# A cross-covariance attention and gated FFN kernel: the second chunk of v transposed by DMA, with four smaller moves

## The chip, the core and the metric

The kernel runs on one core of one Trainium2 chip. The metric is device time in microseconds of one execution. The core has a matrix engine (TensorE, PE in the profile, its weight loads shown as PEld), VectorE (DVE), ScalarE (ACT), GpSimd (POOL) and SyncE (SP), each with its own instruction queue that runs in order. Transfers are issued from a queue (here POOL's, SP's, at the start and the end also ACT's) and carried out by 16 DMA engines. Matmuls write to PSUM, which holds eight banks of 128 x 512 float32 values; the kernel's pools hand these banks out.

## What is computed

```python
B, N, C = 4, 6016, 256          # DFF = 1536
def _attn_ref(q, k, v, tau):
    qn = q / (np.linalg.norm(q, axis=1, keepdims=True) + 1e-06)
    kn = k / (np.linalg.norm(k, axis=1, keepdims=True) + 1e-06)
    s = kn.transpose(0, 2, 1) @ qn / tau
    s = s - s.max(-1, keepdims=True)
    a = np.exp(s)
    a /= a.sum(-1, keepdims=True) + 1e-09
    return v @ a

def _moe_ref(x, w_gate, w_val, w_out):
    gate = 1.0 / (1.0 + np.exp(-(x @ w_gate)))
    return gate * (x @ w_val) @ w_out
```

The second function is applied to the rows of the first one's result. Attention is over channels: for each of four batches one 256 x 256 matrix `a` comes from the whole of q and k, and then every row of v goes through `a` and through the gated FFN. Inputs and output are float32.

## The kernel before

**Stages.** For a batch, scores (`score`, tile ps_s) add up over 47 row tiles of 128 rows; the squares of q and k add up beside them for the norms. Then come the norms, their inverses, the exponentials (`e_sb`) and the row sums. `a` is never applied to v: `gh` multiplies the exponentials with the two weight matrices, giving G and H (12 pieces of 128 x 512, six tiles gh_G0..2 and gh_H0..2), and scales them by the row sums. After that each chunk of four row tiles (512 rows; 12 chunks a batch, the last with three tiles) runs 12 slots. One slot (`glu`) is two matmuls for the gate (ps_gate), two for the value (ps_val), a tanh on ScalarE (g_sb, L501) and one VectorE instruction that makes a slice of hT (L502). The output product of a chunk runs in the slots of the next chunk (`run_work`); all but the first chunk use a scheme of seven products of sums, whose sums VectorE makes (L524, in slots 1, 3, 4, 5, 6 and 7 to 11 of a chunk) and whose results ScalarE copies and GpSimd adds up (L578 to L580, L585, L595, L596). Most matmuls go through one helper, so their line is L127.

**Order.** The order is written out by hand (`manual_schedule`). In the main loop, a slot first issues `glu`, then the sums and a share of the output product, and then the side work that `side_work` has put down for this slot number. Slot numbers count from the start of a batch, 12 a chunk. The side work of a batch holds the loads and transposes of the coming chunks of v, and the whole preparation of the next batch: its loads, scores and squares up to slot 96, then, from `s0` = 98, its norms (`norms_mm`, `root_seed`, `root_steps`), inversion (`norms_inv`, L352 and L353 on VectorE), the spread of the inverse along columns (`spread_both`, four float32 matmuls into ps_rk), a copy of that on ScalarE (`copy_rk`, L315), the scaling of the scores (`scale_x`, L291, two halves), the exponentials (`exps`), the row sums and `gh`.

**The opening.** Batch 0 has nothing to overlap with. POOL's queue issues the loads of q and k (`load_qk`), then the first chunk of v (`load_v(0, 0)`, L178), six pieces of w_gate and w_val (L184), the second chunk of v (L188) and w_out (L195). After the last scores and the norms, TensorE's queue holds: two spreads into ps_rk, eight transposes of the first chunk of v against an identity (L468, tile ps_tp in a bank of the pool psv), the row sum of the first half of the exponentials, the first `gh`, the other row sum, three more `gh` (the second two in psv), and the first `glu`. VectorE copies one half of ps_tp to SBUF (L475), ScalarE the other (L723); the inversion of the first row sum stands ahead of VectorE's half, by way of the `then` argument of `transpose_v`.

**Transposes of v.** Each chunk of v is needed transposed (vT). Chunks from the third on are transposed by a DMA that SP issues (L465, DMA_TRANSPOSE), put down in slot 2 of the chunk before. The second chunk is transposed on TensorE in slot 8 of the first chunk, into a bank of the pool psm, and copied by one VectorE instruction.

**Banks.** Pools psg (ps_gate), psv (ps_val) and pso (ps_o) have two banks each, pss (the scores ps_s) and psm (small things) one.

Of the kernel before, what the change touches and what calls it, by code (L numbers as in the profile page):

```python
# [10 lines left out]
BF16 = mybir.dt.bfloat16  # L11
# [42 lines left out]
def kernel(  # L54
# [21 lines left out]
    P = nc.NUM_PARTITIONS  # L76
# [4 lines left out]
    B, N, C = q.shape  # L81
# [3 lines left out]
    CB = C // P  # L85
# [3 lines left out]
    TPC = 4  # L89
# [7 lines left out]
    def rows(x, b):  # L97
        return x[b].rearrange("(p t) c -> p t c", p=P)
# [3 lines left out]
    def pool(name, bufs, **kw):  # L102
        return ctx.enter_context(tc.tile_pool(name=name, bufs=bufs, **kw))
# [15 lines left out]
    psv = pool("psv", 2, space=PSUM)  # L119
    pso = pool("pso", 2, space=PSUM)  # L120
    pss = pool("pss", 1, space=PSUM)
    psm = pool("psm", 1, space=PSUM)
# [3 lines left out]
    def mm(out, lhsT, rhs, start, stop, **kw):  # L126
        nc.tensor.matmul(out, lhsT=lhsT, rhs=rhs, start=start, stop=stop, **kw)  # L127
# [4 lines left out]
    def load_qk(b, t0, nt):  # L132

        tiles = []
        for name, src in (("q", q), ("k", k)):
            tl = qkpool.tile([P, 2 * TPC, C], BF16, tag=name, name=name + "_sb")
            nc.gpsimd.dma_start(out=tl[:, :nt, :], in_=rows(src, b)[:, t0 : t0 + nt, :])
            tiles.append(tl)
        for u in range(0, nt, TPC):
            qk[b, t0 + u] = [tl[:, u : u + TPC, :] for tl in tiles]  # L140
# [3 lines left out]
    def load_v(b, ci):  # L144
        t0, nt = groups[ci]
        v_sb = vpool.tile([P, TPC, C], BF16, tag="v", name="v_sb")
        nc.gpsimd.dma_start(out=v_sb[:, :nt, :], in_=rows(v, b)[:, t0 : t0 + nt, :])
        vs[b, ci] = v_sb
# [26 lines left out]
    nc.scalar.copy(qk[0, 0][1], first_f32[1])  # L175
    for t0, nt in loads0[1:]:
        load_qk(0, t0, nt)
    load_v(0, 0)  # L178

    w_sb = [[consts.tile([P, CB, FG], BF16, name=f"w_{n}{fg}") for fg in range(NFG)] for n in ("gate", "val")]  # L180
    w_out_sb = consts.tile([P, FC, C], BF16)
    for fg in range(NFG):
        for w, src in enumerate((moe_w_gate, moe_w_val)):
            nc.gpsimd.dma_start(  # L184
                out=w_sb[w][fg],
                in_=src.rearrange("(t p) f -> p t f", p=P)[:, :, ds(fg * FG, FG)],
            )
    load_v(0, 1)  # L188

    w_sums = consts.tile([P, len(B_SUMS), FC // 2, P], BF16)  # L190
# [24 lines left out]
    def invert(out, x, eps, num):  # L215
        nc.vector.tensor_scalar(out=out, in0=x, scalar1=eps, scalar2=None, op0=ALU.add)
        nc.vector.reciprocal(out, out)
# [179 lines left out]
    def row_sums(b, i0, ni, pl, tag):  # L397
        s = st[b]
        ps_r = pl.tile([P, ni], FP32, tag=tag, name="ps_r")
        for i in range(ni):  # L400
            for j in range(CB):
                mm(
                    ps_r[:, i : i + 1],
                    s["e"][i0 + i][:, j, :],
                    ones_bf[:, 0:1],
                    start=(i == 0 and j == 0),
                    stop=(j == CB - 1),
                    skip_group_check=True,
                )
        r = attp.tile([P, ni], FP32, tag=f"rrow{i0}", name="rrow", bufs=2)  # L410
        invert(r, ps_r, 1e-9, 1.0)
        s.setdefault("rrow", []).extend(r[:, i : i + 1] for i in range(ni))
# [6 lines left out]
    def gh_tiles(b):  # L419
        st[b]["gh"] = [  # L420
            [ghpool.tile([P, CB, FG], BF16, tag=f"{n}{fg}", name=f"gh_{n}{fg}") for fg in range(NFG)]
            for n in ("G", "H")
        ]
# [28 lines left out]
    def gh(b, n, pl, tag, act=None):  # L452
        gh_store(b, n, gh_mms(b, n, pl, tag), n % 2 == 0 if act is None else act)
# [1 line left out]

    vts = {}

    def transpose_v(b, ci, ps=None, late=None, then=None):

        t0, nt = groups[ci]  # L460
        v_sb = vs.pop((b, ci))
        vT = vtpool.tile([P, TPC * CB, P], BF16, tag="vT", name="vT")
        flat = v_sb[:, :nt, :].rearrange("p t c -> p (t c)")
        if ps is None:
            nc.sync.dma_start_transpose(out=vT[:, : nt * CB, :], in_=flat)  # L465
        else:
            for n in range(nt * CB):
                nc.tensor.transpose(  # L468
                    out=ps[:, n, :], in_=flat[:, ds(n * P, P)], identity=ident_bf
                )  # L470
            half = nt * CB // 2 if late else nt * CB
            if late:
                late(vT[:, half : nt * CB, :], ps[:, half : nt * CB, :])
                then()
            nc.vector.tensor_copy(out=vT[:, :half, :], in_=ps[:, :half, :])  # L475
        vts[b, ci] = vT.rearrange("p (u cb) n -> p cb u n", cb=CB)

# [203 lines left out]
    for g, (t0, nt) in enumerate(groups0):  # L681
# [6 lines left out]
        while adds:  # L688
            w, last_sq = adds.pop()
# [26 lines left out]
    weights(0, 0)  # L716
    weights(0, 1)
    late = []
    ps_tp = psv.tile([P, TPC * CB, P], BF16, tag="v", name="ps_tp")
    gh_tiles(0)  # L720
    transpose_v(0, 0, ps_tp, lambda *a: late.append(a), lambda: row_sums(0, 0, 1, psm, "m"))
    gh(0, 0, psg, "g", act=True)
    nc.scalar.copy(*late.pop())  # L723
    half_row(0)
# [6 lines left out]
    def side_work(b):  # L731


        side = {}

        def at(slot, fn, *a):
            side.setdefault(divmod(slot, FC), []).append((fn, a))

        for ci in range(NCH):
            nb, nci = (b, ci + 1) if ci + 1 < NCH else (b + 1, 0)  # L740
            lb, lci = (b, ci + 2) if ci + 2 < NCH else (b + 1, ci + 2 - NCH)
            if (nb, nci) == (0, 1):
                at(8, lambda: transpose_v(0, 1, psm.tile([P, TPC * CB, P], BF16, tag="m", name="ps_tp")))
            elif nb < B:
                at(ci * FC + 2, transpose_v, nb, nci)
            if lb < B:
                at(ci * FC + 0, load_v, lb, lci)
            if (b, ci) == (0, 0):
                for i in range(FC // TPC):
                    at(8, copy_w_out, i)  # L750
                for n, m in enumerate((1, 0, 3, 2, 4)):
                    for i in range(FC // TPC):
                        at(10 + 2 * n, sum_w_out, m, i)
        n = b + 1
        if n == B:
            return side
        first, last = (14 if b == 0 else 0), 8 * FC
        for g, (t0, nt) in enumerate(groups):
            s0 = first + g * (last - first) // NCH
            if b == 0:  # L760
                at(max(0, s0 - 12), load_qk, n, t0, nt)
            elif s0 >= 24:
                at(s0 - 24, load_qk, n, t0, nt)
            for u in range(nt):
                at(first + (t0 + u) * (last - first) // NT, score, n, t0, u)
            if g == 0:
                at(s0, acc_start, n)
            for i, (fn, w) in enumerate(((acc_square, 0), (acc_add, 0), (acc_square, 1), (acc_add, 1))):
                at(s0 + 1 + 2 * i, fn, n, g, w)
        if n + 1 < B:  # L770
            for g, (t0, nt) in enumerate(groups[:3]):
                at(NCH * FC - 24 + 8 * g, load_qk, n + 1, t0, nt)
        s0 = 8 * FC + 2
        at(s0, norms_mm, n)
        at(s0 + 1, root_seed, n)
        at(s0 + 1, root_steps, n)
        at(s0 + 9, norms_inv, n)
        at(s0 + 10, spread_both, n)
        at(s0 + 11, copy_rk, n)
        at(s0 + 12, scale_x, n, 0)  # L780
        at(s0 + 13, scale_x, n, 1)
        at(s0 + 14, exps, n, 0)
        at(s0 + 15, exps, n, 1)
        at(s0 + 17, row_sums, n, 0, CB, psm, "m")
        at(s0 + 19, half_row, n)
        at(s0 + 17, gh_tiles, n)
        for i in range(len(gh_order)):
            at(s0 + 18 + 5 * i // 2, gh, n, i, *((pss, "s"), (psm, "m"))[i % 2])
        return side
# [68 lines left out]
```

## Time and profile before

| | |
|---|---|
| median of 4 runs | 809.05 us (808.88 to 809.21) |
| the profiled execution | 808.88 us |
| its span, first to last instruction | 807.1 us |
| mean granted TensorE clock | 0.998 |
| busy: PE, DVE, ACT, POOL | 786.7, 708.9, 525.7, 355.6 us |
| stretch 39 to 47 us: PE, DVE busy | 7.94, 6.57 of 8 us |
| stretch 47 to 56 us: PE, DVE busy | 9.00, 7.09 of 9 us |

The span runs from the first to the last instruction; the time of the execution also has what lies around it, 1.8 us here. A line of the timeline gives the start in us from the beginning of the span, the duration in us, the engine, the source line, the operation, out<-in, the shapes and the number of merged instructions, and in brackets how long the engine was idle before and what ended that. The end of a matmul is modelled and overlaps the next one's start; what TensorE loses is therefore read from the starts of matmuls, gate to gate. In a list of waits a line gives who waited for whom, us in total, times, and the longest. In the DMA view the number at the end of a line is the time from issue to landing.

### The profile page before, as it was taken

How to read it: one execution, taken by the hardware profiler on the slowest of the kernel's cores; microseconds unless marked ns; L12 is line 12 of the kernel's file. 1: busy time of each engine (PE TensorE's matmuls, PEld its weight loads, DVE VectorE, ACT ScalarE, POOL GpSimd, SP SyncE). 2: the span in 40 equal slices, each digit the busy share in tenths (PEclk: the TensorE clock that was granted, in tenths of full speed). 3: DMA queues.
4: the chain of work that ended last, by engine and by line, in shares of the span. 5: the costliest groups of instructions: out<-in, count | busy, mean ns of one | idle time of the engine just before them, and what ended most of it. 6: DMA issues, size and time to landing. Idle time of an engine off the chain costs nothing.

```text
span 807.1 us, 17902 instructions
## 1 busy us (share of the span) xinstructions
PE 786.7 (97%) x6776; PEld 501.0 (62%) x6776; DVE 708.9 (88%) x1202; ACT 525.7 (65%) x891; POOL 355.6 (44%) x566
## 2 busy tenths in 40 slices
PE   4899999999999999999999999999999999999998
PEld 2556666666666666666666666666666566666666
DVE  5777999999879999998987999999988898898896
ACT  3667777766667776775666767776666665665664
POOL 4473545444552454335343544443534244444433
PEclk9999999999999999999999999999999999999999
DMA  9997759432567557422367486524222332432312
GB/s 214 206 207 98 129 93 139 94 67 47 104 128 125 86 108 139 86 53 67 72 119 131 75 142 112 105 54 91 62 53 54 86 66 61 86 65 66 79 34 74
DMA packets 77319, 78.24 MB, mean 97 GB/s; under 512 B 50736, under 2 KB 55088, under 8 KB 77232
## 3 DMA queue, kind: packets, MB, share of 16 engines
q0 software_dynamic: 21648, 39.59, 30.0%
q1 hardware_dynamic: 55008, 36.64, 20.3%
q8 instruction: 53, 0.87, 0.4%
q10 hardware_dynamic: 576, 0.85, 0.3%
q14 instruction: 34, 0.28, 0.1%
HBM read 78.64 MB, written 24.64 MB: 128 GB/s over the span
## 4 chain that ended last, share of the span: by engine, by line
PE 92%; DMA 4%; DVE 2%; ACT 1%; issue 1%; POOL 0%; POOLq 0%
PE ps_gate L127 29%; PE ps_val L127 29%; PE ps_o L127 27%; PE ps_s L127 4%; DMA k_sb<-in_k_dram 3%; PE ps_gh L127 2%; DMA w_gate<-in_moe_w_gate_dram 1%; DVE hT L502 1%; DVE sums L524 0%; ACT g_sb L501 0%; PE ps_rk L127 0%; DVE r L352 0%; DVE acc L278 0%; PE ps_end L127 0%; PE ps_n L127 0%
## 5 line engine op out<-in xcount | busy, mean ns | idle before, releaser
L501 ACT ACTIVATE g_sb<-ps_gate 128x512 f32<-128x512 f32 (+1 forms) x576 | 338.3, 588 | 228.5 <-PE ps_gate L127 220.6
L502 DVE SCALAR_TENSOR_TENSOR hT<-g_sb,ps_val 128x512 bf16<-128x512 f32 (+1 forms) x576 | 384.8, 671 | 79.2 <-ACT g_sb L501 69.6
L127 PE MATMUL ps_val<-vT,gh_H 128*128 128x512 bf16 (+1 forms) x1152 | 337.5, 375 | 0.3 <-DVE hT L502 0.3
L127 PE MATMUL ps_gate<-vT,gh_G 128*128 128x512 bf16 (+1 forms) x1152 | 337.5, 375 | 0.0
L524 DVE TENSOR_TENSOR sums<-hT 128x768 bf16<-128x768 bf16 (+1 forms) x460 | 278.0, 604 | 0.0
L127 PEld LDWEIGHTS <-sums 128*128 128x128 bf16 x2670 | 183.0, 98 | 82.1
L127 PEld LDWEIGHTS <-gh_H 128*128 128x128 bf16 x1152 | 112.7, 98 | 131.6 <-issue 0.8
L595 POOL TENSOR_TENSOR out_sb<-out_sb,m_sb 128x256 f32<-128x256 f32 x89 | 78.6, 884 | 234.1 <-ACT out_sb L585 205.5
L127 PE MATMUL ps_o<-w_sums,sums 128*128 128x128 bf16 x1602 | 154.4, 219 | 0.0
L127 PEld LDWEIGHTS <-hT 128*128 128x128 bf16 x1200 | 88.3, 98 | 46.8
L579 POOL TENSOR_TENSOR m_sb<-m_sb 128x128 f32<-128x128 f32 x89 | 42.2, 474 | 166.0 <-ACT m_sb L578 166.0
L127 PEld LDWEIGHTS <-gh_G 128*128 128x128 bf16 x1152 | 97.0, 98 | 14.9
L127 PE MATMUL ps_o<-w_out_sb,sums 128*128 128x128 bf16 x1068 | 96.2, 219 | 0.0
L127 PE MATMUL ps_o<-w_sums,hT 128*128 128x128 bf16 x1068 | 95.5, 219 | 0.0
L127 PE MATMUL ps_s<-k_sb,q_sb 128*128 128x256 bf16 x376 | 70.7, 292 | 13.7 <-DMA k_sb<-in_k_dram 6.9
L596 POOL TENSOR_TENSOR out_sb<-out_sb 128x256 f32<-128x256 f32 x89 | 76.5, 859 | 7.0
L585 ACT COPY out_sb<-ps_o 128x512 f32<-128x512 f32 x89 | 52.2, 586 | 12.7 <-PE ps_o L127 10.1
L278 DVE TENSOR_TENSOR acc<-acc,sq 128x1024 bf16<-128x1024 bf16 (+1 forms) x66 | 59.8, 906 | 0.0
L580 POOL TENSOR_TENSOR m_sb<-m_sb 128x128 f32<-128x128 f32 x89 | 54.4, 612 | 7.0
L240 ACT ACTIVATE sq<-k_sb 128x1024 bf16<-128x1024 bf16 (+2 forms) x44 | 44.8, 1027 | 12.0 <-DMA k_sb<-in_k_dram 12.0
L127 PEld LDWEIGHTS <-q_sb 128*128 128x128 bf16 x376 | 33.7, 104 | 19.8 <-issue 9.5
L578 ACT COPY m_sb<-ps_o 128x384 f32<-128x384 f32 x89 | 42.6, 479 | 3.4 <-PE ps_o L127 1.0
(78 smaller groups left out, 306.5 us busy)
## 6 DMA issues: line engine op xcount, KB each, us to landing
out_dram<-out_sb SPq DMA_DIRECT2D x43, 512.0 KB, 3.4
v_sb<-in_v_dram POOLq DMA_DIRECT2D x44, 256.0 KB, 5.3
q_sb<-in_q_dram POOLq DMA_DIRECT2D x35, 256.0 KB, 4.9
k_sb<-in_k_dram POOLq DMA_DIRECT2D x35, 256.0 KB, 7.0
q_sb<-in_q_dram POOLq DMA_DIRECT2D x4, 512.0 KB, 11.4
k_sb<-in_k_dram POOLq DMA_DIRECT2D x4, 512.0 KB, 13.3
w_f<-in_moe_w_out_dram POOLq DMA_DIRECT2D x3, 512.0 KB, 10.6
out_dram<-out_sb SPq DMA_DIRECT2D x3, 384.0 KB, 2.8
```

Of the source, the lines that this page charges most:

```text
L127: nc.tensor.matmul(out, lhsT=lhsT, rhs=rhs, start=start, stop=stop, **kw)
L240: nc.scalar.activation(out=sq[:, :nt, :], in_=src[:, :nt, :], func=ACT.Square)
L278: nc.vector.tensor_tensor(out=acc[:, :nt, :], in0=acc[:, :nt, :], in1=st[b]["sq", w][:, :nt, :], op=ALU.add)
L501: nc.scalar.activation(out=g_sb[:, :n], in_=ps_gate[:, :n], func=ACT.Tanh, scale=0.5)
L502: nc.vector.scalar_tensor_tensor(out=hts[b, ci][:, f, :n], in0=g_sb[:, :n], scalar=1.0, in1=ps_val[:, :n], op0=ALU.add, op1=ALU.mult,)
L524: nc.vector.tensor_tensor(out=sums[b, ci, g][:, m, :, : half * P], in0=hT[:, f0 + k0 : f1 : 2, ds(r0 * half * P, half * P)], in1=hT[:, f0 ...
L578: nc.scalar.copy(m, states[p]["ps"][:, : 3 * P].rearrange("p (n c) -> p n c", c=P))
L579: nc.gpsimd.tensor_tensor(out=m[:, 1, :], in0=m[:, 1, :], in1=m[:, 2, :], op=ALU.add)
L580: nc.gpsimd.tensor_tensor(out=m[:, 2, :], in0=m[:, 1, :], in1=m[:, 0, :], op=ALU.add)
L585: nc.scalar.copy(o[:, p : p + half + 1 : half, :], states[p]["ps"].rearrange("p (t c) -> p t c", c=C),)
L595: add(out=ends, in0=ends, in1=states[p]["m"][:, 1:3, :], op=ALU.add)
L596: add(out=ends, in0=ends, in1=mids, op=ALU.subtract)
```

## The change

It has five parts.

- The second chunk of v is transposed by DMA like the later ones, from slot 2 of the first chunk, and not by TensorE in slot 8.
- In the opening, POOL issues the first piece of w_gate ahead of the first chunk of v.
- The first chunk's transposes write to the bank of the pool pss (which ps_s held) and not to one of psv.
- The row sum of the first half, and so its inversion on VectorE, is issued after the first half of the copy of ps_tp, and not before it.
- For batches 1 to 3, inversion, spread and the copy of the spread come one slot later; the first half of the scaling moves from s0 + 12 to s0 + 13, where the second half is.

```diff
@@ opening, loads @@
-    load_v(0, 0)
...
             nc.gpsimd.dma_start(
                 out=w_sb[w][fg],
                 in_=src.rearrange("(t p) f -> p t f", p=P)[:, :, ds(fg * FG, FG)],
             )
+            if fg == 0 and w == 0:
+                load_v(0, 0)
     load_v(0, 1)
@@ transpose_v @@
-    def transpose_v(b, ci, ps=None, late=None, then=None):
+    def transpose_v(b, ci, ps=None, late=None):
...
             if late:
                 late(vT[:, half : nt * CB, :], ps[:, half : nt * CB, :])
-                then()
             nc.vector.tensor_copy(out=vT[:, :half, :], in_=ps[:, :half, :])
@@ opening, transposes @@
-    ps_tp = psv.tile([P, TPC * CB, P], BF16, tag="v", name="ps_tp")
+    ps_tp = pss.tile([P, TPC * CB, P], BF16, tag="s", name="ps_tp")
     gh_tiles(0)
-    transpose_v(0, 0, ps_tp, lambda *a: late.append(a), lambda: row_sums(0, 0, 1, psm, "m"))
+    transpose_v(0, 0, ps_tp, lambda *a: late.append(a))
+    row_sums(0, 0, 1, psm, "m")
     gh(0, 0, psg, "g", act=True)
@@ side_work @@
-            if (nb, nci) == (0, 1):
-                at(8, lambda: transpose_v(0, 1, psm.tile([P, TPC * CB, P], BF16, tag="m", name="ps_tp")))
-            elif nb < B:
+            if nb < B:
                 at(ci * FC + 2, transpose_v, nb, nci)
...
-        at(s0 + 9, norms_inv, n)
-        at(s0 + 10, spread_both, n)
-        at(s0 + 11, copy_rk, n)
-        at(s0 + 12, scale_x, n, 0)
+        at(s0 + 10, norms_inv, n)
+        at(s0 + 11, spread_both, n)
+        at(s0 + 12, copy_rk, n)
+        at(s0 + 13, scale_x, n, 0)
         at(s0 + 13, scale_x, n, 1)
```

## The prediction

> **What bounds the kernel now.** I read the page's chain of waits first, then the list of who waited for whom on TensorE, then timelines around those places.
>
> ```profile
> PE 92%; DMA 4%; DVE 2%; ACT 1%; issue 1%; POOL 0%; POOLq 0%
> ...
> PE ps_rk L127 <- DVE r L353: 1.9, 3, 0.6
> ```
>
> The chain that sets the end is TensorE for 92% of the span. What can still be taken away is TensorE work, or one of the few places where TensorE stands still. One such place is listed: the matmuls that spread the inverted norms (ps_rk) waited three times, once for each later batch. The timeline of the first of them (start, duration in us, engine, line, operation):
>
> ```profile
> 184.96 0.59 PE L127 MATMUL ps_gate<-vT,gh_G 128*128 128x512 bf16 x2
> ...
> 185.57 0.55 DVE L524 TENSOR_TENSOR sums<-hT 128x768 bf16<-128x768 bf16 x1
> ...
> 185.83 0.88 POOL L595 TENSOR_TENSOR out_sb<-out_sb,m_sb 128x256 f32<-128x256 f32 x1 [1.47 <-ACT out_sb L585]
> 186.04 0.69 DVE L352 TENSOR_SCALAR r<-r 128x4 f32<-128x4 f32 x1
> 186.77 0.18 DVE L353 RECIPROCAL r<-r 128x4 f32<-128x4 f32 x1
> 186.78 0.73 POOL L596 TENSOR_TENSOR out_sb<-out_sb 128x256 f32<-128x256 f32 x1
> ...
> 187.00 0.71 PE L127 MATMUL ps_rk<-ident_f,r 128*128 128x128 f32 x4 [0.62 <-DVE r L353]
> ...
> 187.55 0.59 PE L127 MATMUL ps_gate<-vT,gh_G 128*128 128x512 bf16 x2
> ```
>
> See that L352, an addition over four columns, took 0.69 us and ended at 186.73, just after POOL's L595 (186.71). The other two batches show the same 0.69. In the opening the same instruction takes 0.17 (33.20 below). So it waits for POOL's addition, and TensorE waits for it.
>
> The opening, where loads decide:
>
> ```profile
> 26.79 0.53 POOL L147 DMA_DIRECT2D v_sb<-in_v_dram  x1 [0.47 <-DMA q_sb<-in_q_dram]
> ...
> 28.10 0.72 POOL L184 DMA_DIRECT2D w_gate<-in_moe_w_gate_dram  x1 [0.78 <-DMA k_sb<-in_k_dram]
> ...
> 33.20 0.17 DVE L352 TENSOR_SCALAR r<-r 128x4 f32<-128x4 f32 x1 [0.55 <-ACT r L320]
> ...
> 36.03 0.59 PE L127 MATMUL ps_gh<-w_gate,e_sb 128*128 128x512 bf16 x2
> ...
> 37.87 0.59 PE L127 MATMUL ps_gh<-w_val,e_sb 128*128 128x512 bf16 x2 [0.34 <-ACT vT L723]
> ...
> 38.30 0.59 PE L127 MATMUL ps_gate<-vT,gh_G 128*128 128x512 bf16 x2
> ```
>
> By the DMA view v's first chunk lands 6.7 us after its issue (33.49) and the first w_gate 7.9 after (35.99); ps_gh starts 0.04 later. At 37.87 TensorE waits for ScalarE's half of the vT copy, because the fourth ps_gh needs the psv bank that the transposes filled.
>
> The second chunk:
>
> ```profile
> 48.79 11.47 SPq L465 DMA_TRANSPOSE vT<-v_sb  x2
> ...
> 49.74 0.61 PE L468 MATMUL ps_tp<-ident_bf,v_sb 128*128 128x128 bf16 x8
> ...
> 52.78 0.59 PE L127 MATMUL ps_gate<-vT,gh_G 128*128 128x512 bf16 x2
> ```
>
> 52.78 is the first matmul that needs vT of the second chunk. 48.79 is the transpose of the third chunk, issued when its v landed. What its neighbours take, from the DMA view (issue to landing in us at the end of a line; q1 with packets, MB, share of 16 engines in 51.8 to 52.8):
>
> ```profile
> v_sb<-in_v_dram POOLq DMA_DIRECT2D x1, 256.0 KB, 9.9
> ...
> k_sb<-in_k_dram POOLq DMA_DIRECT2D x1, 256.0 KB, 10.1
> ...
> vT<-v_sb SPq DMA_TRANSPOSE x1, 7.1
> ...
> vT<-v_sb SPq DMA_TRANSPOSE x1, 8.6
> ...
> q1 hardware_dynamic: 422, 0.11, 76.7%
> ```
>
> The first is v's second chunk, issued at 33.34, so landed at 43.24. The second is batch 1's first k, issued at 41.26, landed at 51.36. The 7.1 belongs to the transpose at 48.79, the 8.6 to the longest among those I opened (127.28); without loads beside them three took 3.1.
>
> **The change, part by part.**
>
> *Second chunk by DMA.* TensorE loses eight transposes. Gate to gate is 0.86 us in slots before (48.02 to 48.88) and 48.88 to 50.19 = 1.31 with them: **-0.45**. VectorE loses a 0.68 copy at 50.75, worth nothing, since TensorE works on without a gap there. SP gains one DMA_TRANSPOSE (1.2 to 1.4 us of issue) ahead of the third chunk's; SP has nothing else until its first store at 70.29. The transpose goes out when v lands, 43.27, and must land by 52.78-0.45 = 52.33, so it has 9.1 us. With the 7.1 of its nearest neighbour it lands at 50.4, with 8.6 at 51.9: hidden. Against that: the neighbour of 48.79 shows no q1 packets in the windows from 48.8 to 51.8, and its first come at about the landing of that k (51.36). If a transpose stands behind the loads issued before it, ours waits for the same k and lands 2 to 4 us after 51.4, 1 to 3 us late. Ends: -0.45 and +2.6. I take -0.45 with a mean lateness of 0.25 for the overlap of the two: **-0.2**. Its 256 KB push back the loads behind it by some 1.5 us: third chunk's v (48.8, its vT needed after 66), batch 1's first q and k (51.4, first score at 56.68), w_out (cast from 44.84 to 48.8, first used at 53.64). All keep over 2 us.
>
> *Inversions, spread and copy one slot later.* A slot is 1.25 us. Without a stall the 184.96 gate would have been followed by the next at 186.21, where ps_rk began at 187.00: 0.79 lost, three times. In the new place VectorE reaches L352 after hT of the next slot. That hT starts when g_sb ends (186.25), and the next instruction starts some 0.61 later, as it does elsewhere in this timeline: 186.86. This slot has no L524. But POOL's second addition has begun by then: L596 comes 0.80 to 0.95 after L595's start, so from 186.63 or 186.78, and lasts 0.73: to 187.36 or 187.51. If L352 waits again, ps_rk starts 0.29 after that (186.71 to 187.00): 187.65 or 187.80. TensorE gets to it one slot later, at 187.46. Lost 0.19 to 0.34, say 0.26; gain 0.53, three times: **-1.6**. Ends: L352 gets in ahead, -2.37; or it also waits for POOL's next DMA issue (v, 187.46 for 0.62), then ps_rk at 188.37, lost 0.91, +0.36 in all. The row against that last end is 33.20: L352 took 0.17 in the middle of POOL's issue of w_val (32.64 for 0.73).
>
> The Trainium skill (SBUF — State Buffer, "Who interferes with whom") says that whichever of a VectorE instruction in a two-port mode and a GpSimd instruction comes first holds the shared port pair for its whole length, and counts the writing of DMA descriptors among GpSimd's uses. By that rule the load's issue could hold L352 off as well, and the inversions would bring +0.36 where the row of 33.20 gives -1.6. The row decides for me, since it is this very instruction beside such an issue.
>
> *Both scale_x in one slot.* The second delays what follows on VectorE by 0.40 (L291 at 192.70, hT at 193.10). That hT then ends at 194.17 and not 193.77; the matmul into its ps_val bank starts at 194.25. Behind it stand the exponentials on ScalarE, 0.4 later, with the row sums needing them only at 196.33. **0** by 0.08 us of cover; without it 0.4 each, +1.2.
>
> *Load order, bank, copy ahead of the row sum.* w_gate takes v's place and v lands where w_gate did. One engine was held for about 0.94 us by an instruction fetch just then (q8, 9.8% of 16 engines in 33.4 to 34.0), so v is expected at 33.49+1.3+0.94 = 35.75; ends 34.8 (no fetch in its way) and 36.3. The transposes now need ps_s read too (L370 ends at 34.57): earlier, so free. Behind them on TensorE wait the row sum and the first ps_gh. From 35.75: transposes to 36.4, copy 0.41 and inversion 0.36 on VectorE to 37.0 or 37.2, ScalarE's gh_G and vT copy (1.16 plus 0.3 tail less overlap, as from 36.66 to 37.82) to 38.15 or 38.4, gate at 38.2 to 38.45 against 38.30. The stall at 37.87 is gone, but what came behind it is held by the same copy. **+0.05**, ends -0.5 and +0.6.
>
> **Sum**: -0.2 -1.6 +0 +0.05 = -1.75. It is made against the profiled execution, 808.88 for its span of 807.1, which lies 0.17 under the median of the runs. On the median: 809.05-1.75 = 807.3; with the transpose simply on time 807.05. I say **807.2**.
>
> **The rivals.**
>
> 1. *Stall fully gone.* POOL's second addition starts after L352. For it: only 0.08 us lie between the two at the later start. Against: L595 to L596 is as short as 0.80 in the same timeline. -2.37-0.45+0.05 = -2.77 gives 806.3.
>
> 2. *Given back.* Inversions held by POOL's addition and by the load's issue: 809.05-0.45+0.36+0.05 = 809.0. Or the crowded slot costs its 0.4 three times: 807.05+1.2 = 808.25. Or the transpose is 1 to 2 us late: 808 to 809. About 808.5 for the three. For it: VectorE is 88% busy, with 0.08 us of cover in that slot. Against: the 0.17 at 33.20.
>
> 3. *Slower.* The second chunk's transpose stands behind the loads that were issued before 43.3, and TensorE stands at the first gate of that chunk. If it starts at 51.4 and takes as long as the fourth chunk's (issued 58.8, first q1 packets in the window 60 to 61, landed 65.9: 4.9 us), it lands at 56.3, 4.0 late: 807.05+4.0 = 811.05. It decides from 2.0 us of lateness on (landing 54.3, 11 us after issue). For it: the three windows without q1 packets, and that the loads run without a pause from 43 to 50. Against: no transpose that I opened took more than 8.6.
>
> **Chances and range.** About 0.2% (1.6 us) is what a measurement of this kernel can tell from no change, so faster means under 807.43, slower over 810.67. Forecast (806.6 to 807.9) 46%, seven in ten of it under 807.43; rival 1 10%; rival 2 26%; rival 3 18%, five in six of it over 810.67. Faster 0.32+0.10+0.02 of rival 2 = 0.44; slower 0.15; same the rest, 0.41. The range, 806.2 to 809.6, holds the forecast, rivals 1 and 2 and the small end of rival 3; what it leaves out is the rest of that one and a few hundredths below rival 1.
>
> **What would show it.** No L468 for the second chunk, a DMA_TRANSPOSE on SP near 43.3 that lands before that chunk's first gate, and no wait there; L352 still near 0.6 and ending with POOL's L596, ps_rk losing 0.2 to 0.3; gates after the crowded slot at their 1.25 us; the first ps_gh behind the transposes and not behind w_gate. I am wrong if ps_rk still loses 0.8, or if TensorE stands at the second chunk.

## The result, and the profile after

The changed kernel takes 808.19 us (median of 33 runs) against 809.06 (53 runs): a ratio of 0.999, interval 0.9985 to 0.9995. It is 0.87 us faster, about half of the 1.85 that was forecast. The profiled execution took 807.75.

The median hides something that the kernel before does not have. Its runs lie within 0.8 us (808.79 to 809.56). Those of the changed kernel fall into two groups: 17 from 807.40 to 808.19, and 16 from 808.57 to 809.43, with none between. The median, 808.19, is the highest run of the lower group, so the 0.87 us depends on how the runs share out: the lower group's own median is 807.55, the upper one's 808.9. The profiled execution belongs to the lower group. So there are two questions: what the parts brought in the lower group, and what lifts the other half by some 1.3 us.

From the page of the changed kernel, and from its list of waits on TensorE (us in total, times, longest):

```profile
span 806.0 us, 17889 instructions
...
PE 92%; DMA 4%; DVE 2%; issue 1%; ACT 1%; POOL 0%; ACTq 0%; POOLq 0%
```

```profile
PE ps_tp L469 <- DMA v_sb<-in_v_dram: 1.9, 1, 1.9
PE ps_rk L127 <- DVE r L354: 0.5, 3, 0.2
...
PE ps_gate L127 <- ACT vT L724: 0.2, 1, 0.2
```

(L353 and L354 are L352 and L353 of the kernel before.) The wait of the spread has shrunk from 1.9 to 0.5 us. A new one has come: the first transposes wait 1.9 us for v. No wait for the second chunk's vT is listed. The timeline at the first of the three spreads:

```profile
186.48 0.59 PE L127 MATMUL ps_gate<-vT,gh_G 128*128 128x512 bf16 x2
...
187.06 0.73 POOL L596 TENSOR_TENSOR out_sb<-out_sb 128x256 f32<-128x256 f32 x1
...
187.15 0.66 DVE L353 TENSOR_SCALAR r<-r 128x4 f32<-128x4 f32 x1
...
187.84 0.18 DVE L354 RECIPROCAL r<-r 128x4 f32<-128x4 f32 x1
...
188.08 0.71 PE L127 MATMUL ps_rk<-ident_f,r 128*128 128x128 f32 x4 [0.18 <-DVE r L354]
...
188.62 0.59 PE L127 MATMUL ps_gate<-vT,gh_G 128*128 128x512 bf16 x2
```

The addition of four columns still takes 0.66 us, and still ends (187.81) just after a GpSimd addition (187.79), now the second of the pair. The gate at 186.48 and one slot of 1.25 put the spread at 187.73; it starts at 188.08. So 0.35 is lost where 0.79 was: 0.44 gained, and the other two batches show the same. And GpSimd's next DMA issue, 187.72 for 0.62, did not hold the addition: it ended 0.09 us into that issue.

The opening:

```profile
28.24 0.56 POOL L147 DMA_DIRECT2D v_sb<-in_v_dram  x1 [0.60 <-DMA k_sb<-in_k_dram]
...
36.37 0.62 PE L469 MATMUL ps_tp<-ident_bf,v_sb 128*128 128x128 bf16 x8 [1.87 <-DMA v_sb<-in_v_dram]
...
37.02 0.42 DVE L475 COPY vT<-ps_tp 128x512 bf16<-128x512 bf16 x1 [1.46 <-PE ps_r L127]
...
37.80 0.69 ACT L447 ACTIVATE gh_G<-ps_gh,rrow 128x512 bf16<-128x512 f32 x1 [1.63 <-DVE rrow L217]
...
38.39 0.58 ACT L724 COPY vT<-ps_tp 128x512 bf16<-128x512 bf16 x1
...
39.02 0.59 PE L127 MATMUL ps_gate<-vT,gh_G 128*128 128x512 bf16 x2 [0.20 <-ACT vT L724]
...
43.36 1.33 SPq L466 DMA_TRANSPOSE vT<-v_sb  x1
...
53.05 0.59 PE L127 MATMUL ps_gate<-vT,gh_G 128*128 128x512 bf16 x2
```

v lands at 36.34 (28.24 and the 8.1 us of the DMA view). Then everything follows in a row: transposes, VectorE's copy after all eight of them, the inversion behind the copy, ScalarE's gh_G behind that, its own copy of vT, and the first gate at 39.02, where it was at 38.30. The second chunk's transpose takes 9.4 us to land, at 52.76, 0.29 before the first gate that needs it.

### The profile page after: what moved, and what is told of

Read it like the earlier page. It is cut to its first block, busy times and chain, and to the rows that moved or that the text cites. A ratio compares the mean times of both kernels' runs of the same rounds, so it can differ in the third digit from the quotient of the medians.

```text
span 806.0 us, 17889 instructions
## 1 busy us (share of the span) xinstructions
PE 784.5 (97%) x6768; PEld 499.4 (62%) x6768; DVE 706.5 (88%) x1201; ACT 525.3 (65%) x891; POOL 356.0 (44%) x566
## 3 DMA queue, kind: packets, MB, share of 16 engines
q1 hardware_dynamic: 56064, 36.91, 20.7%
## 4 chain that ended last, share of the span: by engine, by line
PE 92%; DMA 4%; DVE 2%; issue 1%; ACT 1%; POOL 0%; ACTq 0%; POOLq 0%
PE ps_val L127 29%; PE ps_gate L127 29%; PE ps_o L127 27%; PE ps_s L127 4%; DMA k_sb<-in_k_dram 3%; PE ps_gh L127 2%; DMA v_sb<-in_v_dram 1%; DVE hT L502 1%; ACT g_sb L501 0%; PE ps_rk L127 0%; DVE r L353 0%; DVE acc L279 0%; DVE sums L524 0%; PE ps_end L127 0%; PE ps_n L127 0%
## 5 line engine op out<-in xcount | busy, mean ns | idle before, releaser
L127 PE MATMUL ps_s<-k_sb,q_sb 128*128 128x256 bf16 x376 | 68.7, 284 | 15.5 <-DMA k_sb<-in_k_dram 8.7
```

## The experiments

Two theories for the two groups went into the first four runs. *Half clock:* TensorE now stands still from 34.5 to 36.4, and in some runs the granted clock falls for a while afterwards. For it: many runs of the upper group list a mean clock of 0.996, those of the lower mostly 0.998. *Transpose at its limit:* with 0.29 us to spare, the second chunk's vT comes late in some runs.

**e1_inv: the later slots alone.**

```diff
-        at(s0 + 9, norms_inv, n)
-        at(s0 + 10, spread_both, n)
-        at(s0 + 11, copy_rk, n)
-        at(s0 + 12, scale_x, n, 0)
+        at(s0 + 10, norms_inv, n)
+        at(s0 + 11, spread_both, n)
+        at(s0 + 12, copy_rk, n)
+        at(s0 + 13, scale_x, n, 0)
```

> The kernel before with the later slots of inversion, spread, copy and scaling alone. In the profile of the changed kernel ps_rk starts 0.45 us earlier against its neighbours in each of three batches (1.33 in all) and no gate after the crowded slot is late. Both theories of the spread of the changed kernel's times (half clock in the opening, or a transpose that lands at its limit) leave this kernel out: 809.05 - 1.3 = 807.7, all runs within 0.7 us as before. If the crowded slot costs after all in most runs, 808.5 and more.

Measured: 807.61 (807.48 to 807.93, 11 runs), ratio 0.9982 (0.9973 to 0.9991): -1.47 against the 809.08 beside it, one group. This part alone brings more than the whole change.

**e2_tp: the DMA transpose alone** (the special case for the second chunk taken out of `side_work`).

> The kernel before with the DMA transpose of the second chunk alone. In the changed kernel it took 9.4 us to land. With the old opening the first gate of the chunk is due at 52.3, so a transpose issued at 43.3 that takes 9.4 is 0.4 late. Half-clock theory: the runs lie close together, at 808.6 if the transpose is on time and 809.0 if it is 0.4 late. Theory of the transpose at its limit: the runs spread over 1 to 2 us as in the changed kernel, and those with the higher times show TensorE waiting at the second chunk's first gate.

Measured: 809.00 (808.70 to 809.29), ratio 0.9999 (0.999 to 1.0008): no difference, one group. Its list of waits has the reason:

```profile
PE ps_gate L127 <- DMA vT<-v_sb: 0.3, 1, 0.3
```

The 0.45 us of transposes saved are given back in a wait of 0.3 in the profiled run. The transpose was late here, and still the runs lie within 0.6 us. That goes against the second theory.

**e3_open: the opening alone** (load order, bank, row sum behind the copy).

> The kernel before with the three parts in the opening alone (load order, bank of the first transposes, row sum behind the copy). Read off the profile of the changed kernel the first gate is 0.72 us later, 0.14 of that from before the opening's reordered part: 809.6 to 809.8. Half-clock theory: two groups of runs, one near 809.7 and one 1.3 higher with a lower granted clock. Theory of the transpose at its limit: one group near 809.7, since the second chunk is transposed by TensorE here.

Measured: 809.42 (808.47 to 811.30), ratio 1.0009 (1.0001 to 1.0018). Seven runs at or below 809.61, four from 810.48 to 811.30. The second chunk is transposed on TensorE here, so the second theory can't make this. The profiled run is one of the four. Its busy time in stretches of 2 us (stretch, its length, busy time of PE, PEld, DVE, ACT, POOL, granted clock, DMA share, GB/s):

```profile
34.00:36.00 2.00, 0.31 (x3) 0.12 (x2) 1.28 (x4) 1.34 (x3) 0.65 (x1) 1.00 1.18 194
36.00:38.00 2.00, 1.94 (x15) 1.19 (x16) 0.78 (x4) 0.17 (x1) 1.51 (x2) 0.58 1.24 205
38.00:40.00 2.00, 2.00 (x7) 0.72 (x6) 0.95 (x3) 1.44 (x4) 0.55 (x1) 0.57 1.24 204
```

and in the profiled run of the changed kernel, of the lower group:

```profile
34.00:36.00 2.00, 0.49 (x4) 0.30 (x3) 1.46 (x4) 1.34 (x3) 0.84 (x2) 1.00 1.21 203
36.00:38.00 2.00, 1.64 (x17) 1.05 (x18) 0.87 (x5) 0.37 (x2) 1.40 (x2) 1.00 1.25 206
38.00:40.00 2.00, 1.79 (x9) 0.71 (x8) 1.50 (x2) 1.97 (x5) 0.66 (x2) 1.00 1.23 203
```

The third column from the right is the clock. After the gap that ends at about 36 it stands at 0.58 and 0.57 in the first and at 1.00 in the second. A mean of 0.58 over 2 us is 1.7 us at half speed, so the two make 3.4 us. The matmuls show it: pairs of ps_gh take 1.01 us where they took 0.59, and the first gate comes at 39.98.

**e4_no_open: the changed kernel with the old opening.**

> The changed kernel with the opening put back as it was, so inversions and DMA transpose alone. Half-clock theory: one group of runs at about 809.05 - 1.3 - 0.45 + 0 to 0.4 late = 807.3 to 807.7, below the changed kernel's median of 808.19. Theory of the transpose at its limit: the transpose has 0.6 us less time than in the changed kernel, so more runs than there are high, median 808 to 809, spread over 1 to 2 us.

Measured: 807.59 (807.35 to 808.01), ratio 0.9982 (0.9973 to 0.9991), one group. Taking back the opening takes the upper group away, with the DMA transpose still there (9.3 us to land, a wait of 0.2).

**e5_busy: TensorE kept at work in the gap.** One line in the changed kernel, ahead of the first transposes:

```diff
+    busy(8)
     late = []
     ps_tp = pss.tile([P, TPC * CB, P], BF16, tag="s", name="ps_tp")
```

> The changed kernel with eight matmuls of constants (0.216 us each, 1.7 in all) ahead of the first transposes, in the stretch from 34.4 to 36.3 in which TensorE waits for v. Nothing else changes, and no result uses them. Half-clock theory: with TensorE busy in that stretch the upper group of runs (808.6 to 809.4) goes away or shrinks to one or two, and the median falls from 808.19 to about 807.5 to 807.7. Rival (the upper group comes from something else, such as where the second chunk's transpose lands): still about half of the runs above 808.5.

Measured: 807.55 (807.39 to 807.92, 11 runs), ratio 0.9982 (0.9973 to 0.9991). No run in the upper group, where it was 16 of 33. In its profile:

```profile
34.00:36.00 2.00, 2.00 (x12) 0.88 (x10) 1.34 (x4) 1.34 (x3) 0.72 (x1) 1.00 1.22 203
36.00:38.00 2.00, 1.98 (x20) 1.18 (x20) 1.05 (x6) 0.50 (x2) 1.48 (x2) 1.00 1.24 205
```

Together with the profile of e3_open that settles the question for the half clock: eight matmuls that compute nothing, in time in which TensorE waits anyway, make the median 0.64 us shorter than the changed kernel's. e7_load, below, was measured in the same session against the same runs of the kernel before, and it has an upper group: a session without half clock is not the reason.

**e6_bank and e7_load: two parts of the opening, each alone.**

```diff
-    ps_tp = psv.tile([P, TPC * CB, P], BF16, tag="v", name="ps_tp")
+    ps_tp = pss.tile([P, TPC * CB, P], BF16, tag="s", name="ps_tp")
```

> The kernel before with the first transposes in the bank of the pool pss alone, loads in the old order. The fourth ps_gh no longer waits for ScalarE's copy of vT (0.34 us of idle time, 0.5 from start to start), so the first gate comes at 37.9 and not 38.3: 808.65, one group. If something behind it (the landing of the second w_gate at 38.15, or VectorE) takes this back: 809.05.

> The kernel before with w_gate ahead of v alone. v lands at 36.0 to 36.3, the transposes wait for it, and the copies of ps_tp, with the bank of the pool psv held until they are done, come behind: first gate 0.7 to 0.9 later, lower group 809.7 to 809.9. Half-clock theory: a second group 1.3 above it with a lower granted clock in some of the runs. Rival: one group.

Measured: the bank alone 808.41 (808.34 to 808.67), ratio 0.9992 (0.9983 to 1.0001), -0.64, one group, first gate at 37.81. The load order alone 809.52 (809.37 to 810.87), ratio 1.001 (1.0002 to 1.0019); seven runs up to 809.64 and four from 810.58 to 810.87, these with a mean clock of 0.995 or 0.996. Alone, the bank is a gain and the load order is a loss, and the loss comes with the second group. Its lower group costs 0.4, less than the 0.7 to 0.9 expected. Together the two do not add up: the lower group of e3_open, which has both, lies at 809.36 and that of e7_load at 809.48, so behind the late v little is seen of the bank's gain. The row sum's new place was not tried alone.

**e8_inv9_spread11: the spread later, the inversion left early.**

```diff
         at(s0 + 9, norms_inv, n)
-        at(s0 + 10, spread_both, n)
-        at(s0 + 11, copy_rk, n)
-        at(s0 + 12, scale_x, n, 0)
+        at(s0 + 11, spread_both, n)
+        at(s0 + 12, copy_rk, n)
+        at(s0 + 13, scale_x, n, 0)
```

> The kernel before with the spread, its copy and the first half of the scaling one slot later, but the inversion left in its old slot. If what TensorE waits for is the inversion held up by GpSimd's addition, the inverse is ready 0.5 us before the spread now and nothing is lost in three batches: 0.79 x 3 = 2.4 off, 806.7. If the spread waits for something else, or if the crowded slot costs without a stall before it, 807.6 as with the inversion moved too.

Measured: 806.53 (806.31 to 806.61, 5 runs), ratio 0.9968 (0.9955 to 0.998): -2.5.

```profile
186.26 0.70 DVE L352 TENSOR_SCALAR r<-r 128x4 f32<-128x4 f32 x1
186.44 0.59 PE L127 MATMUL ps_gate<-vT,gh_G 128*128 128x512 bf16 x2
...
186.99 0.18 DVE L353 RECIPROCAL r<-r 128x4 f32<-128x4 f32 x1
...
187.69 0.66 PE L127 MATMUL ps_rk<-ident_f,r 128*128 128x128 f32 x4
```

The addition waits for GpSimd as before (0.70), but nobody waits for it: the spread starts one slot of 1.25 after the gate at 186.44, at 187.69, with no idle time in brackets. The crowded slot costs nothing that can be seen.

**e9_both: e8 and the bank.**

> The kernel before with the inversion left early and the spread later (806.53 alone) and the first transposes in the bank of pss (808.41 alone, 0.64 under the kernel before). The two lie in different stages, so they add up: 806.53 - 0.64 = 805.9. If not additive: 806.5.

Measured: 806.01 (805.86 to 806.26, 5 runs), ratio 0.9963 (0.995 to 0.9977). Alone the two brought 2.52 and 0.64, together they bring 2.95: they add up but for 0.2. This is the fastest version of the study, 3 us under the kernel before and 2 under the changed one, with the second chunk on TensorE and the old load order.

**e10_early_v: e9 with the DMA transpose and an earlier load of the second chunk's v.**

```diff
     for fg in range(NFG):
+        if fg == 2:
+            load_v(0, 1)
         for w, src in enumerate((moe_w_gate, moe_w_val)):
...
-    load_v(0, 1)
```

> The kernel of the run e9_both, with the second chunk transposed by DMA and its v loaded ahead of the last pieces of w_gate and w_val. v then lands near 40.7 and not 43.3, and the transpose is issued 2.6 us earlier. If its time to land is its own (about 9.3 us whatever stands before it), it lands near 50 and TensorE's 0.45 is saved: 805.5. If it waits behind the loads issued before it (the last one before 40.7 is the first q of batch 1, issued near 40.0 and landing near 50), it lands near 51 to 52, about when the first gate is due (51.8): 805.5 to 806. If v's later loads suffer (the last w_gate lands 1.2 us later and is due at 43.1), up to 0.5 more.

Measured: 806.81 (806.17 to 807.12, 6 runs), ratio 0.9971 (0.996 to 0.9983): 0.8 slower than e9. The transpose is issued 2.8 us earlier than in the changed kernel, at 40.60, and lands later, at 53.2. Waits, landing, and the DMA queues from 49 to 50 us (packets, MB, share of 16 engines):

```profile
PE ps_gate L127 <- DMA vT<-v_sb: 1.2, 1, 1.2
```

```profile
vT<-v_sb SPq DMA_TRANSPOSE x1, 12.6
...
q0 software_dynamic: 103, 0.18, 94.4%
q1 hardware_dynamic: 98, 0.03, 17.7%
```

The page's queue lines give a transpose 1056 packets (q1 has 56064 after the change and 55008 before). Counted microsecond by microsecond, they go in three stages. From the issue at 40.60 to 44 there is none. From 44 to 50 there are 460; in the last five of these six microseconds the transpose (q1) gets on at about one packet for each packet of the queued loads (q0), 98 beside 103 in the one shown. The other 596 follow after 50, when the loads thin out. The changed kernel has the same stages: none from 43.36 to 47, then 37, 102 and 91 in the three microseconds to 50, then 500 and 313. What holds the transpose for its first 4 us no run shows. Without loads beside them, transposes landed in 3.1.

The Trainium skill (DMA: Bandwidth & Descriptors, "Queues, rings and completion order") says that each engine takes turns between the queues that have work, packet by packet. The middle stage agrees, with the 98 and 103; the first stage is not explained by it. The transpose's packets are small (98 make 0.03 MB where 103 of the loads make 0.18), so it loses by such turns.

## Why the prediction was right or wrong

- **Direction and bound.** Right: TensorE on the chain for 92% before and after, and what counts is where it stands still. The time lies in the range and among the cases called "same", but for a reason that no rival names: a load's issue that blocks, a crowded slot and a late transpose, which were to bring about 808.5, did not happen in the profile after, and the upper group came from the clock. That the range holds it is luck in part. The lower group, at 807.55, lies in the forecast's own stretch, 806.6 to 807.9.
- **Inversions, -1.6.** Right in mechanism and nearly in size. The same wait came back behind GpSimd's second addition, as worked out. 0.35 was lost each time, where I took 0.26 from a span of 0.19 to 0.34; the trace gives 3 x 0.44 = 1.32, the runs of e1_inv 1.47. The end at which the load's issue also blocks did not happen. e8_inv9_spread11 shows the wait itself to be the cause: with it off the path the whole 2.4 came.
- **Both scale_x in one slot, 0.** Right: gates at 1.25 after it, in e8 too.
- **DMA transpose, -0.2.** e2_tp gives -0.08: right within what can be told. The landing in 7.1 to 8.6 that I leaned towards was too short; 9.3 and 9.4 were measured, between that and the third rival's 13. That rival's mechanism (the transpose stands behind the loads) was half right: for about 4 us no packet of the transpose moves, but then it doesn't wait for the loads to end, it shares with them packet by packet, as e10_early_v and the changed kernel show.
- **Opening, +0.05: the step that failed.** Two things went wrong in it. v was expected at 35.75 with an end at 36.3, and landed at 36.34, 0.14 of that from loads before it; the first gate came at 39.02 and not at 38.2 to 38.45. And I counted TensorE's wait for v at its length only; the sum has no term for the clock. In 16 of 33 runs of the changed kernel, and in 4 of 11 of e3_open and of e7_load, the time is some 1.3 us higher, and the one profile of such a run shows the clock at half for 3.4 us behind the gap. The opening alone measures +0.34 in the median of e3_open.
- **The sum.** Alone, the parts make -1.47 - 0.08 + 0.34 = -1.21; the changed kernel's lower group, with a median near 807.55, makes -1.5. The two delays seem to overlap there: with the first gate 0.7 later, the second chunk's transpose is just in time, and its wait of 0.3 in e2_tp is not listed. The upper group, half of the runs, pulls the median up to -0.87.

The Trainium skill (TensorE: Matmul & The Clock Gate, "What's actually happening") says that TensorE's clock is gated by its activity in a window of 3413 ns that runs freely, at half rate after an idle window. The 3.4 us at half speed agree, and so does the free window.

The clock records of the traces show it, and show more. In the profile of e3_open half speed begins three times: at 26.09 (in the loading of q and k, where the kernel before has such a stretch too), at 36.33 and at 807.74, which is 3 and 229 times 3.413 us after the first. A wholly idle window is more than it takes here: the window of e3_open that ends at 36.33 holds the whole gap of 1.75 us and still has 1.65 us of TensorE work. In the changed kernel's profile an edge of the windows, counted from its own early stretch, falls into the gap, at 35.32; the windows on its two sides have 2.58 and 2.37 us of work, and the clock stays up. Over the twelve profiles, once the clock has come up, windows of 3.41 us with up to 1.4 us of work were followed by half speed and those with 1.7 or more were not; 1.63 (at the end of e1_inv) and 1.65 (here) went different ways, so the limit lies near half a window. Where the edges fall differs from profile to profile, which is why only some runs lose the clock, as far as the profiles tell: a gap of 1.87 us lies whole in one window for (3.41 - 1.87) / 3.41 = 45% of their positions, an estimate that fits 16 of 33.

## What to carry to other kernels

Where a short instruction is held up by another engine and a third one waits for its result, leave it early and move only the one that waits: the spread alone one slot later brought 2.5 us, inversion and spread together 1.5. A wait of 2 us on TensorE in an opening can cost more than 2 us; compare single runs, not only medians, and fill such a gap with matmuls if it can't be closed. A DMA transpose beside queued loads took 9.3 to 12.6 us here, three to four times its 3.1 alone, and issuing it earlier among the same loads did not help.

## What was not expected

The changed kernel's median is worse than that of its best part alone, since two of its five parts (slots and bank: -1.5 and -0.6) are gains when alone, one (load order) is a loss of 0.4 that also brings the second group, and the transpose brings nothing. And a clock change shows only as 0.998 against 0.996 in a run's mean: one stretch of 3.41 us at half speed takes 0.5 x 3.41 / 807 = 0.002 off it, so 0.998 is one stretch, mostly the early one, and 0.996 is two. It took the granted clock in stretches of 2 us to see where they lie.
